# The MLP's 512-column products read and write backwards, and the sums' tiles begin elsewhere

## The chip, the cores and the metric

The kernel runs on one core of a Trainium2 chip. The metric is the device time of one execution in microseconds. A time is given as the median of several runs; a profile is of one execution, and its span reaches from the first to the last instruction of that execution.

## What is computed

The reference is one block of a network on 2048 positions of 640 channels. A condition `c` gives six modulation rows. A layer norm with two of them feeds a state-space convolution, done with Fourier transforms along the sequence; its output, gated, is added to `x`. A second layer norm feeds a gated MLP with 1728 hidden columns, and that output is gated and added again.

```python
x = A_u
mod = (_silu(c) @ w_mod).reshape(c.shape[0], 6, 1, -1)
sa, ca, ga, sb, cb, gb = (mod[:, i] for i in range(6))
h = _layernorm(x) * (1 + ca) + sa
x = x + ga * _A_ref(h, ...)              # convolution
h = _layernorm(x) * (1 + cb) + sb
gate, up = h @ w1, h @ w3                # 640 -> 1728
x = x + gb * ((_silu(gate) * up) @ w2)   # 1728 -> 640
return x
```

## The kernel before

**Two stages.** The first 380 us or so build the convolution's kernel and apply it; the change leaves them alone. After that the MLP runs to the end. Its tiles come from a pool `wq` in SBUF and two pools of PSUM banks of 512 fp32 columns, `psA` (five banks) and `psG` (three); the function `bank` hands them out under the name `ps`.

**Positions and weights.** The 2048 positions are four quarters of 512. Two quarters, "A" and "B", are worked on together, in two rounds (`pair`). A matmul has 128 rows of channels on the partitions, a stationary tile of 128 x 128 weights and a moving tile of 128 x 512, the quarter; its result is a whole bank of 128 x 512. The 640 channels are five blocks `k`; the 1728 hidden columns are 14 tiles `f`, the last of 64 columns, in which gate and up share one tile.

**Three matmuls for one product.** Every operand is split into a high and a low part (`split`, `x_split`, `w_split`: ScalarE casts to the rounded type `F32R`, VectorE takes the difference). `prod3` (line 1241) multiplies high with high, high with low and low with high, all adding up in one bank. These are the names in the trace: `gh`, `gl`, `uh`, `ul` for the parts of gate and up weights (the parts of `w2` and of the hidden tile use the same places), `xA`, `xB` and `T` for moving tiles, `S0h` to `S3l` for sums of weights.

**Strassen blocks.** `seven` computes, for one tile `f` and both quarters, gate and up together with seven block products in place of eight. Four of them need sums or differences of weights, made by `w_sums` (line 1307; GpSimd adds into `S0` to `S3`) and split by `w_split` (ScalarE into `S0h`.., VectorE into `S0l`..) for the next block while the present one is multiplied. Each is a tile of 128 partitions x 2 blocks x 128 columns, of which one block of 128 columns at a time is the stationary tile. `plain` does the tiles that are not done so: four tiles in the first round, one in the second, each for A and for B; the first of them uses an order of its own (`early`, line 1269 on).

**Output product.** `outputs` (line 1386 on) goes over the 14 hidden tiles of a quarter with five banks open. For four of them the hidden tile is stationary and 512 columns of `w2` move; for the fifth 128 columns of `w2` are stationary and the hidden tile moves (line 1455).

**What sets the order.** The program's order on an engine is kept where `in_order` is set or `keep_in_program_order` is called; elsewhere the framework's scheduler orders the instructions, and it puts in all waits. Places in SBUF are given out by the pools from the sizes of the tiles.

Not all 512-column matmuls are in the change: the `idle` ones of `keep_warm` (line 1054) and those of the first stage (line 541) are not.

Of the kernel before, what the change touches and what calls it, by code (L numbers as in the profile page):

```python
# [9 lines left out]
F32 = mybir.dt.float32  # L10
F32R = mybir.dt.float32r
# [6 lines left out]
P = 128  # L18
# [90 lines left out]
def tile_kernel(ctx: ExitStack, tc: tile.TileContext, a):  # L109
    nc = tc.nc  # L110
    V, S, G, PE = nc.vector, nc.scalar, nc.gpsimd, nc.tensor
# [725 lines left out]
    first, rest = Polar(d0, Vo, l2f), Polar(d1, Go, [l2, l2])  # L837
# [81 lines left out]
    for word in FRONT:  # L919
        main, *opts = word.split("/")  # L920
        n = next((int(o) for o in opts if o.isdigit()), 0)
        tag = next((o for o in opts if o in ("A", "B")), "B")
        name, k = main.split("+") if "+" in main else (main, None)
# [5 lines left out]
        else:  # L929
            k = int(k)  # L930
# [41 lines left out]
    for rnd in range(NS // EB + 3):  # L972
        for word in ROUND:
            word, _, idle = word.partition("/")
            name, k = word[:2].rstrip("+-"), EB * rnd + int(word[len(word[:2].rstrip("+-")):])
# [11 lines left out]
    for tk in range(NS - 4, LAG + 8 * NDC + 2):  # L987
        do("st", tk)
        do("kc", tk)
        last = do("iv", tk - 1)  # L990
# [11 lines left out]
        i = tk - 1 - LAG - 8 * NDC + 8  # L1002
# [31 lines left out]
    wq = ctx.enter_context(tc.tile_pool(name="wq", bufs=1, side="right"))  # L1034
    sp_order = [False]
    V, S, G, PE = (InOrder(tc, e, (in_order,)) for e in (V, S, G, PE))
# [204 lines left out]
    def prod3(ps, terms, first, last):  # L1241

        n = len(terms)
        for i, ((wh, wl), (xh, xl)) in enumerate(terms):
            for j, (w, x) in enumerate(((wh, xh), (wh, xl), (wl, xh))):
                ins = PE.matmul(ps, w, x, start=(first and i + j == 0), stop=(last and i == n - 1 and j == 2),
                                skip_group_check=not first)
        return ins

# [9 lines left out]
    def plain(c, f, h, ws, early=False, between=None, then=None):  # L1259

        last = f == NFT - 1
        wgs, wus = ws
        ks = range(KD) if c == "A" else (4, 0, 2, 3, 1)
        x = {k: xop[c, k] for k in ks}
        pg = bank(1)
        if early and f == 0:
            pu = bank(1)
            for lo in range(2):
                for k in range(KD):
                    for ps, ws in ((pg, wgs), (pu, wus)):  # L1270
                        for i in range(1 if lo else 2):
                            end = PE.matmul(ps, ws[i][:, k, :], x[k][lo], start=(k + i + lo == 0),
                                            stop=(lo == 1 and k == KD - 1))
        else:
            end = prod3(pg, [(wk(wgs, k), x[k]) for k in ks], True, True)
            if between:
                with tc.issue_after(end.ins):
                    between()
            if not last:
                pu = bank(1)  # L1280
                terms = [(wk(wus, k), x[k]) for k in ks]
                if then:
                    end = prod3(pu, terms[:3], True, True)
                    with tc.issue_after(end.ins):
                        then()
                    end = prod3(pu, terms[3:], False, True)
                else:
                    end = prod3(pu, terms, True, True)
        sg = room(8)
        if not last:  # L1290
            S.activation(sg, pg, AF.Silu)
            made[0] = V.tensor_tensor(h, pu, sg, op=OP.mult)
        else:
            S.activation(sg[:64], pg[:64], AF.Silu)
            made[0] = V.tensor_tensor(h[:64], pg[64:], sg[:64], op=OP.mult)
        return end
# [5 lines left out]
    def block_split(W):  # L1302
        W[2] = split(W[0], WS, ("gh", "gl"))
        W[3] = split(W[1], WS, ("uh", "ul"), part=slice(2, KD))
        return W

    def w_sums(W, names):

        wg, wu, _, _, sums = W
        for n in names:  # L1310
            t = (wq.tile([P, 2, P], F32, name=f"S{n}"), wq.tile([P, 2, P], F32R, name=f"S{n}h"),
                 wq.tile([P, 2, P], F32R, name=f"S{n}l"))
            raw = lambda i: sums[i][0]
            l, r = (lambda: (wu[:, :2], wu[:, 2:4]), lambda: (raw(0), wg[:, :2]),
                    lambda: (wg[:, :2], wu[:, :2]), lambda: (wg[:, 2:4], raw(1)))[n]()
            G.tensor_tensor(t[0], l, r, op=OP.subtract if n else OP.add)
            sums[n] = t
# [68 lines left out]
    def outputs(q0, order, hs, side, last):  # L1386


        seq = [(c, f) for c in range(2) for f in order]
        n_all, raws, ops, xr, accs, late = len(seq), {}, {}, [], [], []  # L1390

        def load(n):
            if n < n_all:
                raws[n] = weight(seq[n][1], "w2")

        def gate(n):

            if last and NFT <= n < n_all:
                V.tensor_tensor(raws[n][:, :512], raws[n][:, :512], gbr, op=OP.mult)

        def operands(n):
            if n < n_all:
                c, f = seq[n]
                ops[n] = out_operands(raws.pop(n), hs[c][f], f)

        def tail(tiles, ob, x, g):

            pt = bank(g)
            for i in tiles:
                PE.transpose(pt[:, i * P:(i + 1) * P], ob[:, i * P:(i + 1) * P], ident)  # L1410
            for i in tiles:
                V.tensor_tensor(x[i][:, 512:], pt[:, i * P:(i + 1) * P], x[i][:, 512:], op=OP.add)

        def finish(i, q, ob, x, gated, g):

            tail((i,), ob, x, g)
            V.tensor_tensor(x[i][:, :512], gated[i], x[i][:, :512], op=OP.add)
            x_out(4 * q + i, x[i])

        in_order[0] = True  # L1420
        for n in range(5):
            load(n)
        operands(0)
        in_order[0] = False
        yield
        in_order[0] = True
        for n, (c, f) in enumerate(seq):
            q, pos = q0 + c, n % NFT
            operands(n + 1)
            load(n + 5)  # L1430
            gate(n + 3)
            if pos == 10:
                xr = [x_tile(), x_tile()] + ([x_tile(), x_tile()] if c or last else [x_place("T41"), x_place("T31")])
                for i in range(4):
                    SQ.dma_start(xr[i], xs[4 * q + i])
            if pos == 0:
                acc = {k: bank(0) for k in (4, 0, 1, 2, 3)}
            side(n)
            terms = ops.pop(n)
            run = [(k, terms) for k in (4, 0, 1, 2, 3)]  # L1440

            if c and last and pos == NFT - 2:
                held, run = terms, run[:3]
            if c and last and pos == NFT - 1:
                run[3:] = [(k, held + terms) for k in (2, 3)]
            if pos == NFT - 1:
                if c == 0:
                    gated, ob = [room(4 + i) for i in range(4)], room(8)
                elif last:
                    ob = room(8)  # L1450
                else:
                    *gated, ob = places(3) + places(3)[:2]
            for k, terms in run:
                for i, (hh, w) in enumerate(terms):
                    lhs, rhs = (hh[:, k * P:(k + 1) * P], w[:, :512]) if k < 4 else (w[:, 512:], hh)
                    PE.matmul(acc[k], lhs, rhs, start=(pos == 0 and i == 0),
                              stop=(pos == NFT - 1 and i == len(terms) - 1))
                if pos < NFT - 1:
                    continue

                if k == 4:
                    S.activation(ob, acc[4], AF.Copy, scale=modT[:, 2, 4:5])
                elif not (c and last):
                    V.tensor_tensor(gated[k], acc[k], gbr, op=OP.mult)
                else:
                    V.tensor_tensor(xr[k][:, :512], acc[k], xr[k][:, :512], op=OP.add)
                    if k == 1:
                        tail(range(4), ob, xr, 1)
                    for i in ((), (0, 1), (2,), (3,))[k]:
                        x_out(4 * q + i, xr[i])  # L1470
            for t in late[:2]:
                t()
            late = late[2:]
            if pos == NFT - 1 and not (c and last):
                late = [lambda i=i, t=(q, ob, xr, gated, 1 - c): finish(i, *t) for i in range(4)]
        side(n_all)
        in_order[0] = False
        yield
        for t in late:
            t()  # L1480
            yield
# [58 lines left out]
    for pair in range(2):  # L1540
# [5 lines left out]
        ws = first_plain.pop() if first_plain else plain_weights(simple[0], last_sum)  # L1546
# [18 lines left out]
        for n, f in enumerate(simple):  # L1565
            hA[f] = h_tile()
            ws = ws or plain_weights(f, ends if pair == 0 and n == 1 else None)
            end = plain("A", f, hA[f], ws, pair == 0, *((lambda: turn(4, 0, 2), lambda: turn(3, 1)) if n == 3 else ()))
            if n < len(simple) - 1:
                ws = None  # L1570
# [111 lines left out]
```

## Time and profile before

| | us |
|---|---|
| median of three runs | 934.82 (934.5 to 937.22) |
| span of the profiled execution | 932.9 |
| TensorE busy | 894.6, 8482 matmuls |
| VectorE busy | 692.8 |
| ScalarE busy | 552.7 |
| GpSimd busy | 282.3 |

In the trace PE is TensorE's matmul, PEld its load of stationary weights (a row of its own, since it overlaps with matmuls), DVE VectorE, ACT ScalarE, POOL GpSimd and SP the queue of SyncE. A row of groups has the line, the engine, the operation, the tiles (written <- read, without buffer numbers), the shapes and the count; then busy time in us and the mean duration of one in ns; then idle time before them. All instructions that go through the helper which keeps the program's order have its line, L103, so that the tiles tell them apart. In a timeline the first number is the start and the second how long the row lasts. Matmuls are pipelined, and one's duration reaches into the next; the step from start to start is the time that each takes from the engine.

### The profile page before, as it was taken

What the parts mean: (1) busy time and instruction counts of PE and PEld (TensorE: products, weight loads), DVE (VectorE), ACT (ScalarE), POOL (GpSimd) and SP (SyncE); (2) the same over time, 40 slices, a digit from 0 to 9 for tenths busy, and PEclk for the clock granted to TensorE, in tenths of its full rate; (3) what the DMA queues carried; (4) which work ended last, traced back from release to release, by engine and by line L of the source; (5) the groups of instructions that cost most, each with busy time, mean ns of one, the idle gap of its engine ahead of it and who ended that gap; (6) DMA issues with size and microseconds to landing.
All of it is one profiled execution on the core that took longest, in us unless ns stands there. A gap on an engine that the chain in (4) does not pass through costs nothing.

```text
span 932.9 us, 21160 instructions
## 1 busy us (share of the span) xinstructions
PE 894.6 (96%) x8482; PEld 699.1 (75%) x8482; DVE 692.8 (74%) x1251; ACT 552.7 (59%) x810; POOL 282.3 (30%) x282
## 2 busy tenths in 40 slices
PE   5999889999999999999999999999999999999998
PEld 3776667767777766678888887778888888888886
DVE  6699889999999967676666656686876766664665
ACT  4899899999999843464433323466643333333432
POOL 3633465555556312134222200111632222200000
PEclk9999999999999999999999999999999999999999
DMA  8755888665655987853113117984322211203453
GB/s 253 243 198 201 264 230 223 171 162 153 177 155 149 230 223 245 211 212 99 56 49 97 55 45 201 271 258 158 86 70 85 84 57 57 57 29 99 141 169 114
DMA packets 103703, 140.79 MB, mean 151 GB/s; under 512 B 20612, under 2 KB 62788, under 8 KB 103604
## 3 DMA queue, kind: packets, MB, share of 16 engines
q1 hardware_dynamic: 99772, 129.32, 47.8%
q0 software_dynamic: 2368, 7.77, 2.6%
q10 hardware_dynamic: 1464, 2.34, 0.8%
q8 instruction: 67, 1.10, 0.5%
q14 instruction: 32, 0.26, 0.1%
HBM read 107.94 MB, written 31.46 MB: 149 GB/s over the span
## 4 chain that ended last, share of the span: by engine, by line
PE 72%; ACT 14%; DVE 5%; DMA 4%; issue 3%; SPq 1%; DVEq 0%; ACTq 0%
PE ps L103 56%; PE p L672 4%; ACT cs L137 3%; PE pz L721 3%; ACT A L137 3%; ACT ph L137 2%; PE pm L103 2%; ACT L137 2%; PE pk L614 1%; PE pq L552 1%; PE pa L541 1%; ACT kc L140 1%; DVE uk L103 1%; SPq L103 1%; ACT uk L140 1%
## 5 line engine op out<-in xcount | busy, mean ns | idle before, releaser
L103 DVE TENSOR_TENSOR s<-ps,s 128x512 f32<-128x512 f32 x138 | 94.9, 687 | 80.2 <-PE ps L103 79.7
L566 POOL TENSOR_TENSOR ph<-thi,iota 128x1024 int32<-128x1024 int32 x40 | 98.0, 2451 | 129.5 <-DVE A L604 77.5
L103 DVE TENSOR_TENSOR gl<-rw,gh 128x640 fp32r<-128x640 f32 x87 | 78.0, 897 | 64.2 <-ACT gh L103 64.2
L103 ACT CAST gh<-rw 128x640 fp32r<-128x640 f32 x87 | 63.3, 727 | 101.8 <-PE ps L103 61.5
L103 POOL TENSOR_TENSOR S<-rw 128x256 f32<-128x256 f32 x46 | 36.6, 798 | 170.7 <-DVE S0l L103 151.5
L103 PE MATMUL ps<-xA,gh 128*128 128x512 f32 x280 | 87.9, 392 | 0.1
L103 PE MATMUL ps<-gh,uh 128*128 128x512 f32 x224 | 87.5, 391 | 0.0
L103 PE MATMUL ps<-gl,uh 128*128 128x512 f32 x224 | 87.2, 389 | 0.0
L103 PE MATMUL ps<-gh,ul 128*128 128x512 f32 x208 | 81.1, 390 | 0.0
L672 PE MATMUL p<-uk,s 128*64 128x256 f32 x640 | 77.1, 383 | 0.9 <-issue 0.9
L103 PEld LDWEIGHTS ps<-xA,gh 128*128 128x128 f32 x280 | 52.1, 188 | 12.8 <-ACT xA L103 0.8
L672 PEld LDWEIGHTS p<-uk,s 128*64 128x64 f32 x640 | 43.4, 137 | 22.5 <-issue 3.4
L103 PE MATMUL ps<-xA,gl 128*128 128x512 f32 x140 | 54.5, 390 | 0.0
L103 ACT ACTIVATE s<-ps 128x512 f32<-128x512 f32 (+1 forms) x33 | 19.7, 598 | 50.5 <-PE ps L103 50.5
L600 DVE TENSOR_TENSOR A<-A,ph 128x1024 f32<-128x1024 f32 x40 | 49.0, 1226 | 0.0
L721 PE MATMUL pz<-Y,i 64*128 64x128 f32 x640 | 45.5, 281 | 3.6 <-ACT zt L140 2.0
L721 PEld LDWEIGHTS pz<-Y,i 64*128 64x128 f32 x640 | 39.3, 187 | 12.8 <-issue 7.3
L593 DVE TENSOR_TENSOR E<-A,cs 128x1024 f32<-128x1024 f32 x40 | 48.6, 1216 | 0.4
L103 PEld LDWEIGHTS ps<-gl,uh 128*128 128x128 f32 x224 | 42.1, 188 | 9.0
L103 PEld LDWEIGHTS ps<-gh,uh 128*128 128x128 f32 x224 | 42.1, 188 | 8.7
L137 ACT ACTIVATE cs<-cs,hp 128x1024 f32<-128x1024 f32 x40 | 45.3, 1153 | 0.2
L570 POOL TENSOR_TENSOR ph<-ph,phi 128x512 int32<-128x512 int32 x40 | 44.5, 1115 | 2.6
(244 smaller groups left out, 2301.6 us busy)
## 6 DMA issues: line engine op xcount, KB each, us to landing
rw<-in_w_dram SPq DMA_DIRECT2D x52, 320.0 KB, 3.0
us<-u SPq DMA_DIRECT2D x16, 640.0 KB, 4.5
s<-in_s_dram SPq DMA_DIRECT2D x40, 256.0 KB, 3.4
i<-in_i_dram SPq DMA_DIRECT2D x40, 256.0 KB, 4.0
rw<-in_wg_dram SPq DMA_DIRECT2D x31, 320.0 KB, 3.0
rw<-in_wu_dram SPq DMA_DIRECT2D x28, 320.0 KB, 3.5
uk<-us SPq DMA_DIRECT2D x32, 256.0 KB, 8.1
zs<-zt SPq DMA_DIRECT2D x32, 256.0 KB, 4.1
```

The lines of the kernel that those rows point to most:

```text
L103: ins = fn(*args, **kw)
L137: return tc.keep_in_program_order(S.activation(*args, **kw))
L140: return tc.keep_in_program_order(S.copy(out, in_))
L541: keep(PE.matmul(pA[s][:, rr, :], la[r, t, :], r2[r, js, :].rearrange("p j b -> p (j b)"), start=True, stop=True, tile_position=(r.start, 0)))
L552: keep(PE.matmul(pQ[s][:, rr, :256], w[r, t, :], bc(sel[r, js], 2, NA) if i else r1[r, js, :], start=(i == 0), stop=(i == 1), tile_positio ...
L566: keep(G.tensor_tensor(p, bc(thi[:, s * SD:s * SD + SD], 2, NPH), bc(iota, 1, SD), op=OP.mult))
L570: keep(G.tensor_tensor(p[:, :, :NA], p[:, :, :NA], bc(phi[:, s * SD:s * SD + SD], 2, NA), op=OP.add))
L593: keep(V.tensor_tensor(EC[s][:, :, 1:3, :], AA[s][:, :, 1:3, :], mid(cs[s]), op=OP.mult))
L600: keep(V.tensor_tensor(A[:, :, 1:3, :], A[:, :, 1:3, :], mid(ph[s]), op=OP.mult))
L614: keep(PE.matmul(pk[dq * 32:dq * 32 + 32, g, :], x[:, g * 4 + dq, 1, :], x[:, g * 4 + dq, 0:3:2, :], start=(st == 0), stop=(st == 1), tile ...
L672: keep(PE.matmul(p2[par * 64:par * 64 + 64, pi, c, :], s2[:, pi * 2 + par, c * 64:c * 64 + 64], uk[:, 0:kn + 1:kn, f, :], start=True, stop ...
L721: ins = keep(PE.matmul(pz[:, par, (g % 2) * 2 + pi, :], i1[r, pi, c, :], Y[r, pi, c, :], start=(c == 0), stop=(c == 1), tile_position=(par ...
```

## The change

In three places, a matmul's output and its moving operand are given with a step of -1 along the columns, `[:, ::-1]`: in `prod3`, in the early part of `plain` and in `outputs`. The last column is read and written first. The result of each column lies where it lay before.

In `w_sums` the eight split tiles of the sums are made by a new function, `shifted`. The table `ROOM` gives for each a number of columns by which the tile is made wider, and the column at which its 256 columns begin. The tile of the unsplit sum is as before.

```diff
-                ins = PE.matmul(ps, w, x, start=(first and i + j == 0), stop=(last and i == n - 1 and j == 2),
+                ins = PE.matmul(ps[:, ::-1], w, x[:, ::-1], start=(first and i + j == 0), stop=(last and i == n - 1 and j == 2),
                                 skip_group_check=not first)
...
-                            end = PE.matmul(ps, ws[i][:, k, :], x[k][lo], start=(k + i + lo == 0),
+                            end = PE.matmul(ps[:, ::-1], ws[i][:, k, :], x[k][lo][:, ::-1], start=(k + i + lo == 0),
                                             stop=(lo == 1 and k == KD - 1))
...
+    ROOM = {"S0h": (8, 1), "S0l": (0, 0), "S1h": (8, 2), "S1l": (0, 0), "S2h": (24, 4), "S2l": (0, 0), "S3h": (40, 0),
+            "S3l": (8, 3)}
+
+    def shifted(name):
+
+        extra, at = ROOM[name]
+        t = wq.tile([P, 2 * P + extra], F32R, name=name)
+        return t[:, at:at + 2 * P].rearrange("p (k c) -> p k c", k=2)
+
     def w_sums(W, names):
...
-            t = (wq.tile([P, 2, P], F32, name=f"S{n}"), wq.tile([P, 2, P], F32R, name=f"S{n}h"),
-                 wq.tile([P, 2, P], F32R, name=f"S{n}l"))
+            t = (wq.tile([P, 2, P], F32, name=f"S{n}"), shifted(f"S{n}h"), shifted(f"S{n}l"))
...
-                    PE.matmul(acc[k], lhs, rhs, start=(pos == 0 and i == 0),
+                    PE.matmul(acc[k][:, ::-1], lhs, rhs[:, ::-1], start=(pos == 0 and i == 0),
                               stop=(pos == NFT - 1 and i == len(terms) - 1))
```

## The prediction

> **What bounds the kernel now.** I read the head of the page, its chain, then the table of windows, the merged chain in order of time, and last the timeline of TensorE inside the last stage.
>
> ```profile
> span 932.9 us, 21160 instructions
> PE 894.6 (96%) x8482; PEld 699.1 (75%) x8482; DVE 692.8 (74%) x1251; ACT 552.7 (59%) x810; POOL 282.3 (30%) x282
> ...
> PE 72%; ACT 14%; DVE 5%; DMA 4%; issue 3%; SPq 1%; DVEq 0%; ACTq 0%
> ```
>
> ```profile
> 500.00:550.00 50.00, 50.00 (x222) 41.42 (x221) 32.27 (x58) 18.89 (x36) 8.89 (x12) 1.00 0.19 54
> 600.00:650.00 50.00, 50.00 (x284) 38.28 (x283) 37.68 (x72) 31.86 (x49) 7.67 (x13) 1.00 0.70 209
> 800.00:850.00 50.00, 50.00 (x223) 41.40 (x222) 27.97 (x46) 17.13 (x31) 2.95 (x4) 1.00 0.19 54
> ```
>
> ```profile
> 416.61 244.49 PE ps L103 x1163
> 661.75 267.25 PE ps L103 x1182
> ```
>
> The last 530 us are one stretch of TensorE work. In the windows the first time after the width is TensorE's busy time, 50.00 of 50 us, at a granted clock of 1.00 (third column from the end), and the merged chain from 416.61 to 929.00 us holds almost nothing but matmuls into the tiles `ps`. VectorE (32.27, 37.68 and 27.97 us of 50) and ScalarE are well below that. So whatever the change does to the time of a 512-column product goes straight into the end; whatever it does to the other engines has to be large to be seen.
>
> How long is one product? Not what the groups give as a mean of one (that is its latency, and neighbours overlap), but the step from one start to the next:
>
> ```profile
> 789.68 0.39 PE L103 MATMUL ps<-xA,gl 128*128 128x512 f32 x1
> 789.90 0.62 PE L103 MATMUL ps<-xA,gh 128*128 128x512 f32 x2
> 790.36 0.39 PE L103 MATMUL ps<-xA,gl 128*128 128x512 f32 x1
> 790.58 0.62 PE L103 MATMUL ps<-T,S0h 128*128 128x512 f32 x2
> 791.04 0.39 PE L103 MATMUL ps<-T,S0l 128*128 128x512 f32 x1
> 791.26 0.62 PE L103 MATMUL ps<-T,S0h 128*128 128x512 f32 x2
> 791.72 0.39 PE L103 MATMUL ps<-T,S0l 128*128 128x512 f32 x1
> 791.94 0.62 PE L103 MATMUL ps<-xB,uh 128*128 128x512 f32 x2
> 792.40 0.39 PE L103 MATMUL ps<-xB,ul 128*128 128x512 f32 x1
> ```
>
> Twelve products start between 789.68 and 792.40: 2.72 / 12 = 226.7 ns a step, the same for `gh`, `uh` and the sums `S0`. The reader is to see that nothing in it wobbles: while VectorE and ScalarE work at two thirds and one third of their time, and transfers run, the step stays the same. Any gain must come out of the step itself.
>
> **How many products the edit touches.** Seven Strassen products a weight block are 54 matmuls (seven of two terms and four of one term more, each term three matmuls), for 23 blocks: 1242. The plain blocks are 240, and the output product 4 x (13 x 15 + 10) = 820. Together **2302**. The 32 `idle` matmuls (line 1054) and the transposes are not touched. 2302 x 226.7 ns is 521.9 us, 56% of the span. One nanosecond a product is 2.3 us, and 0.3% of the kernel is 1.2 ns a product.
>
> **The change, part by part.** It adds no instruction, no transfer and no wait: the same matmuls in the same accumulations, with first and last column exchanged in reading and in writing, so every column meets the same weights. No engine gets another queue. What moves is where a stream begins: at the last column of `x`, `h` or `w2` and of its bank of PSUM, while the load of the next weights begins, as before, at its first.
>
> *Read and write from behind.* The trace of before has no matmul with a descending operand, so this is an unknown, to be bounded. Another engine does read descending in this kernel: lines 596 and 604 take `cs` and `ph` with a step of -1, lines 593 and 600 with +1.
>
> ```profile
> L600 DVE TENSOR_TENSOR A<-A,ph 128x1024 f32<-128x1024 f32 x40 | 49.0, 1226 | 0.0
> L593 DVE TENSOR_TENSOR E<-A,cs 128x1024 f32<-128x1024 f32 x40 | 48.6, 1216 | 0.4
> L596 DVE TENSOR_TENSOR E<-A,cs 128x512 f32<-128x512 f32 x40 | 28.5, 712 | 0.0
> L604 DVE SCALAR_TENSOR_TENSOR A<-ph,A 128x512 f32<-128x512 f32 x40 | 27.5, 702 | 0.0
> ...
> L103 DVE TENSOR_TENSOR s<-ps,s 128x512 f32<-128x512 f32 x138 | 94.9, 687 | 80.2 <-PE ps L103 79.7
> ```
>
> 712 and 702 ns descending stand beside 687 ns for 512 ascending columns (from PSUM): 15 to 25 ns an instruction, none of it a doubling. That speaks against a catastrophe, though VectorE's ports need not be TensorE's.
>
> For the gain, the nearest row is the one stream in the trace that sends 512 columns in another form: line 672, two 64-column halves side by side, 256 columns each.
>
> ```profile
> 249.59 1.95 PE L672 MATMUL p<-uk,s 128*64 128x256 f32 x16
> ```
>
> ```profile
> L672 PE MATMUL p<-uk,s x640: 379/379/431, 129.6 to 362.6; 128*64 128x256 f32 x160
> ```
>
> Sixteen matmuls are eight pairs, 512 columns a pair; less one duration (431 or 379 ns) the 1.95 us leave 1.52 to 1.57 us for seven steps, **217 to 224 ns**. So TensorE passes 512 columns and turns to new weights in 2.7 to 10 ns less than the 226.7 ns of the MLP. Some of that step is a turn-over between two instructions, and not streaming; and the turn-over is what the edit touches, since it moves both ends of every stream. Bounds a product: -10 ns (all of it gone, -23.0 us) on the one side; on the other +6 ns, the spread of the durations of one such product (389 to 395 ns in the row of S1h below), +13.8 us. Between them I take **-3.3 ns**, a third of the 10: nearer to the row of the MLP itself, since a step that is alike for every tile gives no sign that all of it can go. 2302 x 3.3 = **7.6 us** less, all of it on the path.
>
> [...]
>
> *The eight places.* Five of the eight tiles grow, together by 88 elements of 4 bytes in each partition, four begin 1, 2, 4 or 3 elements behind their start, and tiles laid out behind them in the same pool move.
>
> ```profile
> L103 PEld LDWEIGHTS ps<-T,S1h x92: 187/188/188, 439.4 to 824.6; 128*128 128x128 f32 x92
> L103 PE MATMUL ps<-T,S1h x92: 389/389/395, 439.6 to 824.8; 128*128 128x512 f32 x92
> L103 ACT CAST S1h<-S x23: 403/406/408, 427.6 to 813.1; 128x256 fp32r<-128x256 f32 x23
> L103 DVE TENSOR_TENSOR S1l<-S,S1h x23: 408/415/626, 428.0 to 813.9; 128x256 fp32r<-128x256 f32 x23
> ```
>
> A load of these weights takes 188 ns inside a step of 226.7: 38.7 ns are cover, and only what a load from a skew start takes beyond that reaches the path. The sums are 4 x 46 x 3 = 552 of the loads; were they late by 4 ns (nothing shows it), that would be 2.2 us. The casts and differences that write the tiles are done 11 us ahead of their first use (428.0 and 0.4 beside 439.4), so even twice their 0.4 us stays hidden; that cover gone, each of the 23 blocks would pay up to 0.4 us a sum. I cost the places at nothing beyond what they share in the step.
>
> **Sum.** 932.9 - 7.6 = 925.3 us of span. The median of the runs, 934.82, lies 1.9 us above the profiled span; the forecast is 925.3 + 1.9, **927 us**.
>
> **The rivals.**
>
> *Same step.* The turn-over belongs to the exchange of weights in the array and does not see where a stream begins. For it: 226.7 ns for every operand in the timeline above, in and out of the sums. Against it: line 672 turns over faster in the same array, so the turn-over does hang on an instruction's operands. Time: 934.8, give or take 2. The same comes out if the patterns are undone on their way to the chip.
>
> *A dearer step (the other side).* The first columns come late: the stream begins at the end of a row, and reads or writes that profit from going up lose it at each start. Place: the start of each of the 2302 products; price: the 6 ns by which one product may last longer (395 against 389), 13.8 us, **949 us**. It decides from 1.2 ns a product on. For it: VectorE's descending instructions cost 15 to 25 ns more than the ascending one. Against it: VectorE's pair also differs in where its operands lie (PSUM or SBUF), so these may be no price of direction.
>
> *A stream at half speed.* If each descending column takes two slots of the stream in place of one, a product costs up to 226.7 ns more: 2302 x 226.7 = 522 us, some 1457 us. Against it: VectorE's 712 beside 687 ns.
>
> [...]
>
> **How the numbers follow.** Forecast (a shorter step): 0.47, with its own range 911 to 931. Same step: 0.20. Dearer step: 0.28, half speed: 0.05. What a measurement of this kernel can tell from no change is about 0.3%, 2.8 us. Faster by more 0.47, within 0.20, slower by more 0.33. The range reaches from 910 (a little past the whole 10 ns) to 951 (a little past the 6 ns more); I leave some 0.04 below it and 0.14 above.
>
> **What would show it.** In the profile of the changed kernel, the step between starts in the timeline around 790 us: 223 ns by the forecast, 226.7 by the same step, 233 by the dearer, over 400 by half speed; and with it the number of matmuls in the windows of 50 us at full TensorE (222 or 223 now; 225 or 226 by the forecast). If the places matter by themselves, the steps into S0 to S3 differ from those into `gh` and `uh`; if the loads suffer, their 188 ns grow. The forecast is wrong if the step is unchanged and time goes elsewhere: into waits of TensorE on S tiles, or into the first 380 us, which the edit leaves alone.

## The result, and the profile after

| | before | after |
|---|---|---|
| median of the runs, us | 935.66 (934.5 to 937.22, 4 runs) | 947.57 (946.58 to 947.97, 4 runs) |
| span of the profiled execution, us | 932.9 | 946.2 |

The ratio is 1.0133, with a 95% interval of 1.0116 to 1.0149: **slower by 1.3%**, where 927 us had been forecast. In the MLP every engine works through the same instructions in the same order in both profiles.

Two windows of the changed kernel (columns as before: PE, PEld, DVE, ACT, POOL busy with counts, granted clock, share and rate of the transfers), and the end of its merged chain:

```profile
500.00:550.00 50.00, 50.00 (x215) 40.23 (x214) 31.42 (x56) 18.26 (x37) 9.44 (x13) 1.00 0.17 54
800.00:850.00 50.00, 50.00 (x215) 40.23 (x214) 29.91 (x50) 16.85 (x32) 5.88 (x8) 1.00 0.13 39
```

```profile
416.25 526.09 PE ps L103 x2347
```

TensorE is as full as before and its clock is granted as before, but 215 matmuls fit into 50 us where 222 and 223 did. From 416 us on, the same matmuls last 526.1 us in place of 512.4 (416.61 to 929.00), 13.7 us more; the span grew by 13.3. So all of it came from this stretch. The timeline of TensorE in the changed kernel:

```profile
799.77 0.40 PE L103 MATMUL ps<-xA,gl 128*128 128x512 f32 x1
800.01 0.63 PE L103 MATMUL ps<-T,S0h 128*128 128x512 f32 x2
800.47 0.40 PE L103 MATMUL ps<-T,S0l 128*128 128x512 f32 x1
800.71 0.63 PE L103 MATMUL ps<-T,S0h 128*128 128x512 f32 x2
801.17 0.40 PE L103 MATMUL ps<-T,S0l 128*128 128x512 f32 x1
801.41 0.63 PE L103 MATMUL ps<-xB,uh 128*128 128x512 f32 x2
801.87 0.40 PE L103 MATMUL ps<-xB,ul 128*128 128x512 f32 x1
802.11 0.63 PE L103 MATMUL ps<-T,S2h 128*128 128x512 f32 x2
802.57 0.40 PE L103 MATMUL ps<-T,S2l 128*128 128x512 f32 x1
```

Twelve starts in 2.80 us: **233.3 ns a step**, 6.7 ns more than in the timeline of the forecast. Over all products, leaving out the few steps above 300 ns, the mean step is 227.2 ns before and 233.6 after, which is why the 13.7 us are a little less than 2302 x 6.7 = 15.4. The loads of the weights did not grow, those from a tile that begins 8 bytes later among them:

```profile
L103 PEld LDWEIGHTS ps<-T,S1h x92: 188/188/188, 439.7 to 835.1; 128*128 128x128 f32 x92
L103 PE MATMUL ps<-T,S1h x92: 395/398/400, 439.9 to 835.3; 128*128 128x512 f32 x92
```

The steps into the sums differ from the others only a little: products of S1 step by some 235 ns and those of `S3l` by 238, all of it together some 0.4 us.

### The profile page after: what moved, and what is told of

It is laid out like the page before. It is cut to its first block, busy times and chain, and to the rows that moved or that the text cites. A ratio compares the mean times of both kernels' runs of the same rounds, so it can differ in the third digit from the quotient of the medians.

```text
span 946.2 us, 21160 instructions
## 1 busy us (share of the span) xinstructions
PE 906.7 (96%) x8482; PEld 698.8 (74%) x8482; DVE 693.0 (73%) x1251; ACT 552.0 (58%) x810; POOL 277.5 (29%) x282
## 4 chain that ended last, share of the span: by engine, by line
PE 75%; ACT 12%; DVE 7%; issue 3%; DMA 2%; POOL 0%; DVEq 0%; POOLq 0%; ACTq 0%
PE ps L103 58%; PE p L672 5%; PE pz L721 3%; ACT cs L137 3%; ACT A L137 2%; ACT ph L137 2%; PE pk L614 2%; DVE uk L103 2%; ACT L137 1%; PE pm L103 1%; PE pt L633 1%; PE pa L541 1%; PE pq L552 1%; ACT kc L140 1%; DVE E L593 1%
## 5 line engine op out<-in xcount | busy, mean ns | idle before, releaser
L103 DVE TENSOR_TENSOR gl<-rw,gh 128x640 fp32r<-128x640 f32 x87 | 76.0, 874 | 69.3 <-ACT gh L103 69.2
L103 PE MATMUL ps<-xA,gh 128*128 128x512 f32 x280 | 89.9, 400 | 0.1
L103 PEld LDWEIGHTS ps<-gh,ul 128*128 128x128 f32 x208 | 39.1, 188 | 9.4
```

Source lines behind the costliest of these rows:

```text
L103: ins = fn(*args, **kw)
```

## The experiments

### Which part of the change

**The places alone** (`e1_places`): the change without its three reversals.

> The eight places alone; all products stream forwards. Direction theory (the backward stream costs 6.7 ns a product, the places next to nothing): about 935 us, step 226.7 ns everywhere except a few ns more into the shifted sums. Address theory (the step is set by where operands start within 64 bytes; the five wider tiles move every tile of the pool from 32 to 0 modulo 64): the step changes for all products, up or down, and the time with it by 2.3 us per ns.

Measured: 939.67 us, ratio 1.0059 (1.0042 to 1.0076). The timeline around products of a sum:

```profile
785.79 0.62 PE L103 MATMUL ps<-xB,gh 128*128 128x512 f32 x2
...
789.87 0.62 PE L103 MATMUL ps<-T,S1h 128*128 128x512 f32 x2
790.32 0.40 PE L103 MATMUL ps<-T,S1l 128*128 128x512 f32 x1
790.56 0.63 PE L103 MATMUL ps<-T,S1h 128*128 128x512 f32 x2
791.02 0.40 PE L103 MATMUL ps<-T,S1l 128*128 128x512 f32 x1
791.26 0.62 PE L103 MATMUL ps<-xA,gh 128*128 128x512 f32 x2
...
792.63 0.62 PE L103 MATMUL ps<-xA,gh 128*128 128x512 f32 x2
```

Up to 789.87 eighteen products step by 226.7 ns; from there the next twelve need 2.76 us, 230 ns each, and the six behind the last product of S1 are among them (1.37 us, 228 ns each). The places do cost time when the stream goes forwards, 5.3 us by the medians, and they cost it in the stream, though the loads of `S1h` still take 187 to 189 ns.

**The reversal alone** (`e2_reversed`): the three lines with `[:, ::-1]`, tiles as before.

> The backward stream alone; all tiles where they were (32 modulo 64). Direction theory: the step is 233.3 ns everywhere, about 949 us. Address theory: another step than 233.3, since the streams now start at 28 and not at 60 modulo 64 and the weights at 32 and not at 0; anything from 216 to 240 ns, 911 to 966 us.

Measured: 947.61 us, ratio 1.0145 (1.0128 to 1.0162), 216 matmuls in each of the two windows. That is the whole of the change's loss: with the places 1.0133, without them 1.0145, the intervals overlap. The step is the direction's, with the tiles of the change or without them, and the 5 us of the places are not added to it.

**All tiles moved by 32 bytes** (`e3_pad`): one tile is 8 columns wider, so that the pool should lay its tiles elsewhere. The profiles show no addresses; where the tiles lie is worked out from their sizes, here and in the next two runs.

```diff
-                 wq.tile([P, 2, P], F32R, name=f"S{n}l"))
+                 wq.tile([P, 2 * P + 8 * (n == 3)], F32R, name=f"S{n}l")[:, :2 * P].rearrange("p (k c) -> p k c", k=2))
```

> The kernel before with S3l alone 8 columns wider and begun at its first column: every tile of the pool moves by 32 bytes, from 32 to 0 modulo 64, nothing else changes. Direction theory: no change, 935 us. Address theory: another step for all products; by the turn-over seen in line 672 it may fall to 217 to 224 ns, 913 to 929 us.

Measured: 934.25 us, ratio 0.9997 (0.998 to 1.0014). Moving them all together is of no account, if they moved as worked out.

**Which property of the places.** `e10_widths` keeps the wider tiles and begins each at its first column (`return t[:, :2 * P]`); `e11_starts` has the starts of the change, but widths of 0 or 16 columns, so that every tile stays on the old grid of 64 bytes.

> The places alone, forwards, with the wider tiles but all begun at their first column: the sums' weights lie at 0 or 32 bytes modulo 64, no other start. If the 5 us of the places alone came from starts off the 32-byte grid: 934 us. If a change of 32 bytes between one load of weights and the next is enough to unsettle the forward stream: 937 to 940 us, with steps above 230 ns at the products of sums.

> The skew starts alone, forwards: every tile is 64 bytes wider or not at all, so that all tiles stay 32 modulo 64, and only S0h, S1h, S2h and S3l begin 4, 8, 16 and 12 bytes behind. If the skew starts unsettle the forward stream: 937 to 940 us, steps above 230 ns at products of these four, 226.7 elsewhere. If the widths did it: 934 us.

Measured: 937.48 us, ratio 1.0032 (1.0016 to 1.0047), and 939.61 us, ratio 1.0089 (1.005 to 1.0129). Both cost something, 3.5 and 5.6 us by the medians; the runs of the second scatter up to 951.8 us, which lifts its ratio above that of its medians, 1.006. The time is lost around the products of sums: in the profiles the eight kinds of them step by 228 to 235 ns on average in both kernels, where all eight stood at 226.5 to 226.9 before, and the other products by 228 as against 227; the last 1182 products of TensorE's chain take 269.32 and 270.05 us, where 267.25 stood before. In the second kernel the low parts, whose tiles begin where they began, are slower too (232 and 233 ns for `S1l` and `S0l`, which were expected at 226.7). That would fit with a price for every change of the start from one load of weights to the next; this is my guess, and how such a change would reach the stream, no run shows.

**Reading or writing.** `e5_write` turns only the outputs round, `e6_read` only the moving tiles.

```diff
+                ins = PE.matmul(ps[:, ::-1], w, x, ...     # e5_write
+                ins = PE.matmul(ps, w, x[:, ::-1], ...     # e6_read
```

> Only the output of the 2302 products is written backwards; the moving tiles are read forwards (so the columns of every product come out mirrored). Read theory (the dearer step belongs to reading the moving tile backwards): the step is 226.7 ns and the time 934 us. Write theory (it belongs to PSUM): 233.3 ns and 948 us.

> Only the moving tiles are read backwards; PSUM is written forwards (columns mirrored again). Read theory: 233.3 ns, 948 us. Write theory: 226.7 ns, 934 us. If each half costs a part, both kernels lie between.

Measured: 934.49 us for writing (ratio 1.002, 0.9978 to 1.0063) and 948.76 us for reading (1.0135, 1.0065 to 1.0204). The same window of each:

```profile
800.00:850.00 50.00, 50.00 (x223) 41.38 (x222) 28.05 (x46) 16.92 (x31) 2.95 (x4) 1.00 0.17 54
```

```profile
800.00:850.00 50.00, 50.00 (x216) 40.26 (x215) 30.37 (x51) 17.18 (x32) 5.86 (x8) 1.00 0.14 40
```

223 matmuls as before when only PSUM is written backwards, 216 when only SBUF is read backwards. All of the loss is in reading. (A product that is turned round on one side alone has its columns mirrored, so these two kernels do not compute the block.)

**A part of the products** (`e8_outputs`): the third reversal alone, 820 products.

> Backwards in the output product alone, 820 of the 2302 products, places as before. If each backward product costs 6.7 ns on TensorE's path, wherever it stands: 820 x 6.7 = 5.5 us more, 940 us. If the cost arose through the pipelines of the Strassen blocks: no change, 934 us.

Measured: 939.63 us, ratio 1.005 (1.0018 to 1.0082), 5.7 us above its runs of before; the interval leaves room for 1.7 to 7.7 us. Its profile is sharper: the products of the output step by 233 ns or a little more, and those of the Strassen blocks by 227 as before. The price goes with each product.

### What in the reading costs the time

**Ten products, many starts** (`e4_bench`).

> The kernel before with 84 groups of ten 512-column matmuls on zeros ahead of the MLP, each group with another start of the moving tile (M, bytes modulo 64) and of the stationary tile (S), forwards (u) or backwards (d) in reading and writing. Direction theory: all groups uu step alike, about 226.7 ns, all dd alike, about 233. Address theory: the step goes with M and S; groups with one direction spread by several ns, and M32S32uu shows 226.7, M60S0dd 233.3. The mixed groups (ud, du) tell reading from writing.

Backwards in both, nineteen of the twenty groups stepped by 233 ns, whatever their starts; forwards, groups differed. Some rows of its timeline (start, length of the whole group):

```profile
399.48 2.43 PE L189 MATMUL M32S8uu<-T 128*128 128x512 f32 x10
...
436.48 2.47 PE L189 MATMUL M32S32uu<-T 128*128 128x512 f32 x10
...
496.66 2.50 PE L189 MATMUL M60S0dd<-T 128*128 128x512 f32 x10
```

2.43 us less a last duration of 0.39 are nine steps of 226.7 ns, 2.50 less 0.40 nine of 233.3. Ten products proved too few to tell a start from the settling of the stream: M32S32uu, the case of the kernel before, has not reached 226.7 here. It is inconclusive on the starts, and led to groups of thirty.

**Columns, weights, types** (`e7_bench`).

> The kernel before with groups of thirty matmuls on zeros ahead of the MLP: N columns (512, 384, 256), weights of W columns (128, 64, 32), forwards (U) or backwards (D), then two-byte and full fp32 operands, and two groups that write backwards. Cost per stream (the extra arises at a start): D minus U is 6.7 ns at every N. Cost per column: 6.7, 5.0 and 3.3 ns at 512, 384 and 256. [...]

The timeline, from which the step is the distance from one group's start to the next's, by 30:

```profile
381.60 6.96 PE L133 MATMUL N512W128U<-T 128*128 128x512 f32 x30
388.40 7.17 PE L133 MATMUL N512W128D<-T 128*128 128x512 f32 x30
395.41 7.07 PE L133 MATMUL N512W64U<-T 128*64 128x512 f32 x30
402.31 7.17 PE L133 MATMUL N512W64D<-T 128*64 128x512 f32 x30
409.31 7.11 PE L133 MATMUL N512W32U<-T 128*32 128x512 f32 x30
416.26 7.17 PE L133 MATMUL N512W32D<-T 128*32 128x512 f32 x30
...
439.03 5.43 PE L133 MATMUL N384W64D<-T 128*64 128x384 f32 x30
444.30 5.37 PE L133 MATMUL N384W32U<-T 128*32 128x384 f32 x30
...
454.77 3.77 PE L133 MATMUL N256W128U<-T 128*128 128x256 f32 x30
458.38 3.72 PE L133 MATMUL N256W128D<-T 128*128 128x256 f32 x30
461.93 3.59 PE L133 MATMUL N256W64U<-T 128*64 128x256 f32 x30
465.36 3.70 PE L133 MATMUL N256W64D<-T 128*64 128x256 f32 x30
468.90 3.57 PE L133 MATMUL N256W32U<-T 128*32 128x256 f32 x30
...
475.84 6.65 PE L133 MATMUL SHORTW128U<-T 128*128 128x512 bf16 x30
482.33 6.64 PE L133 MATMUL SHORTW128D<-T 128*128 128x512 bf16 x30
...
501.97 26.02 PE L133 MATMUL FULLW128U<-T 128*128 128x512 f32 x60
527.82 25.91 PE L133 MATMUL FULLW128D<-T 128*128 128x512 f32 x60
```

Backwards with 64 columns of weights the steps are 233.3, 175.7 and 118.0 ns for 512, 384 and 256 columns: 57.7 ns for every 128 columns and some 2.6 ns beside them. So a backward stream is paid by the column, and at 512 columns it does not depend on the weights: 7.17 us with 128, 64 and 32 columns of them. D minus U does shrink with the weights (some 7, 3 and 2 ns at 512 columns), as a collision of the stream with the load of the next weights might have it, but since U grows (226.7, 230.0, 231.7 ns) and not because D falls. Forwards there is no such simple line: with 256 columns and 128 of weights U is even dearer than D (120.3 against 118.3 ns). So D minus U, which is what the change paid, follows neither of the two rows that were expected for it, one price per stream or one per column: with 128 columns of weights it is 7 ns at 512 columns, some 3 at 384 and -2 at 256. Of the two groups that write backwards, the one that reads backwards too takes 7.17 us like the others that do, 233.7 ns from start to start (7.01 / 30). The one that reads forwards, first behind the full fp32 groups, takes 7.38 us and 240.7 ns on average (7.22 / 30), so that for writing alone `e5_write` is the better witness.

And two-byte operands know no direction (6.65 and 6.64 us, (6.65 - 0.38) / 29 = 216 ns a step), nor does full fp32, of which the trace lists two passes for each matmul (x60 for thirty): 431 ns a pass (25.85 / 60), the groups lasting 26.02 and 25.91 us. The theory of one price at each start falls, and a collision with the load of the next weights does not show in D, which is the same with 128, 64 and 32 columns of them; of the three types only four-byte operands in a single pass (x30 for thirty) lose by going backwards. No run leaves the loads of weights out, so what part they have in the forward step stays open.

**Other orders of the same columns** (`e9_patterns`).

> The kernel before with groups of thirty matmuls on zeros ahead of the MLP, all with four-byte operands, 512 columns read in other orders: blocks taken from behind with ascending columns inside (BLOCKSDOWN), blocks in order with descending columns inside (INSIDEDOWN), two halves or four quarters in turns (HALVES, QUARTERS), one column again and again (SAME), every second column (STEPTWO), one row of 128 four times (SAMEROW). If the extra comes from fetching the moving tile: SAME falls to the 215.8 ns of two-byte operands, STEPTWO is far above 233, and the orders fall into 226.7 or 233.3 ns by the size of the block at which the direction turns. If it is a rate of the array itself with four-byte operands: SAME stays at 226.7 ns and all orders lie at 226.7 to 233.3. An order below 226.7 ns would beat both kernels.

```profile
388.28 7.17 PE L137 MATMUL DOWNA<-T 128*128 128x512 f32 x30
395.28 7.16 PE L137 MATMUL BLOCKSDOWN2X<-T 128*128 128x512 f32 x30
...
437.11 6.96 PE L137 MATMUL BLOCKSDOWN128X<-T 128*128 128x512 f32 x30
443.91 6.96 PE L137 MATMUL INSIDEDOWN2X<-T 128*128 128x512 f32 x30
...
464.49 8.16 PE L137 MATMUL INSIDEDOWN16X<-T 128*128 128x512 f32 x30
...
493.59 6.64 PE L137 MATMUL HALVES1X<-T 128*128 128x512 f32 x30
500.07 10.17 PE L137 MATMUL HALVES2X<-T 128*128 128x512 f32 x30
...
574.62 6.72 PE L137 MATMUL SAMEA<-T 128*128 128x512 f32 x30
581.18 13.78 PE L137 MATMUL STEPTWOA<-T 128*128 128x512 f32 x30
```

The same products cost from 6.64 to 13.78 us for thirty by nothing but the order in which columns are read. Descending blocks of two cost as much as a stream backwards, descending blocks of 128 nothing; descending pairs inside ascending blocks cost nothing, sixteens inside cost most (266.7 ns). Every second column doubles the step (453.3 ns), and one column again and again takes 218.7. So the step is no fixed rate of the array for four-byte operands. But the orders do not fall into the two steps 226.7 and 233.3 either, as had been expected if it is the fetch, and what rule they follow stays open. And one order is quicker than the kernel before: column 0, 256, 1, 257 and so on, 6.48 / 30 = **216 ns**.

**In turns from two halves, in the kernel** (`e12_turns`). The matmuls read so and write PSUM in order; the last operation behind each product puts the columns back.

```diff
+    turns = lambda v: v.rearrange("p (a c) -> p c a", a=2)
+    paired = lambda v: v.rearrange("p (c a) -> p c a", a=2)
+    halves = lambda v: v.rearrange("p (a c) -> p a c", a=2)
+    back = lambda v: v.rearrange("p (c a) -> p a c", a=2)
...
-                ins = PE.matmul(ps, w, x, start=(first and i + j == 0), stop=(last and i == n - 1 and j == 2),
+                ins = PE.matmul(paired(ps), w, turns(x), start=(first and i + j == 0), stop=(last and i == n - 1 and j == 2),
...
-        V.tensor_tensor(hB, t, c12, op=OP.mult)
+        V.tensor_tensor(halves(hB), back(t), back(c12), op=OP.mult)
...
-                    S.activation(ob, acc[4], AF.Copy, scale=modT[:, 2, 4:5])
+                    S.activation(halves(ob), back(acc[4]), AF.Copy, scale=modT[:, 2, 4:5])
-                    V.tensor_tensor(gated[k], acc[k], gbr, op=OP.mult)
+                    V.tensor_tensor(halves(gated[k]), back(acc[k]), halves(gbr), op=OP.mult)
```

(The other two matmuls, the other products of `seven` and `plain` and the last sum are edited alike.)

> All 2302 products read their moving tile in turns from its two halves (columns 0, 256, 1, 257, ...) and write PSUM in order; the last elementwise operation behind each product puts the columns back. Fetch theory (the step above 215.9 ns is time to fetch four-byte columns): step 215.9 ns, 2302 x 10.8 ns = 24.9 us less than before, 909 us. Turn-over theory (it belongs to the exchange of weights): 226.7 ns, 934 us or some us more for the operations that put columns back.

Measured: **910.38 us** (908.7 to 912.19, 6 runs), ratio 0.9734 (0.9709 to 0.9759). A window, and the last stretch of the chain:

```profile
800.00:850.00 50.00, 50.00 (x234) 43.83 (x233) 26.79 (x39) 18.30 (x30) 0.00 (x0) 1.00 0.28 85
```

```profile
668.73 236.18 PE ps L103 x1097
```

```profile
L103 DVE TENSOR_TENSOR h<-s,s 128x512 f32<-128x512 f32 x24 | 16.4, 683 | 3.1 <-ACT s L103 3.0
L103 DVE TENSOR_TENSOR h<-s,s 128x512 f32<-128x512 f32 x24 | 20.9, 871 | 3.1 <-ACT s L103 3.0
```

234 matmuls in the window, and 236.18 us for the last 1097, 215 ns each: the step of two-byte operands, with every load of weights still there. So the turn-over theory falls. Putting the columns back lengthens VectorE's product of the hidden tile from 683 (first row, the kernel before) to 871 ns (second row), nearly all of it beside work that TensorE covers: it is busy for 49.4 us or more of each 50 from 450 to 900. This kernel beats both.

**With the eight places on top** (`e13_turns_places`), and **more places in turn** (`e14_turns`).

> The same, with the eight places of the change. If the places cost only because they disturb a fetch that is at its limit: no difference to the run without them, 909 us. If the load of weights from skew starts is itself late: some 3 to 5 us more.

> The kernel before with groups of thirty matmuls on zeros ahead of the MLP, read in turns from 2, 4, 8 and 16 places, upwards (U) and downwards (D). Fetch theory, with direction told by neighbours in the stream: in turns no neighbour lies next in memory, so U and D step alike, 215.9 ns at 2. If the direction is told by the whole pattern: D is dearer by up to 6.7 ns. More places may step like 2 or lose again.

The first took 912.63 us, ratio 0.9759 (0.9731 to 0.9786), 2.3 us more by the medians, with an interval that overlaps with the one without the places; its last 1097 products need 236.19 us where the other needs 236.18, so the stream does not see the places. In the second:

```profile
390.27 6.64 PE L116 MATMUL TURNS2UP<-T 128*128 128x512 f32 x30
396.75 6.64 PE L116 MATMUL TURNS2DP<-T 128*128 128x512 f32 x30
403.23 8.66 PE L116 MATMUL TURNS4UP<-T 128*128 128x512 f32 x30
411.72 8.77 PE L116 MATMUL TURNS4DP<-T 128*128 128x512 f32 x30
```

From two halves in turns, upwards and downwards step alike. Four places are slower than a plain stream (283 ns), eight and sixteen slower still (489 and 433 ns), and I have no explanation for that.

## Why the prediction was wrong

**What bounds the kernel: right.** The step of the 512-column products was the only term that moved the end, and the reading of it by start to start, the count of 2302 and the price of 2.3 us a ns hold within what was measured (`e8_outputs`: 820 products, 5.5 us expected, 5.7 measured).

**The step that failed** is the one that took the shorter step of line 672 for a quicker turn-over: "the turn-over is what the edit touches, since it moves both ends of every stream", and from it -3.3 ns. Line 672 multiplies full fp32, not the single-pass four-byte type of the MLP. `e7_bench` has some 430 ns for a pass of 512 columns of that type, in both directions; a pass of 256 columns would be half of it, an estimate of 215 ns. The trace of before bears that out: the starts of the two matmuls of a pair lie 6 to 7 ns apart, and the next pair starts 215 to 216 ns after the last, but for the first step of 267 ns. So the two halves of a pair run side by side, each for the full time of 256 such columns; the 217 to 224 ns were this time with the long first step in the mean, and no stream of 512 columns. And the step of the MLP holds no turn-over of 10 ns: with the same loads and the same exchanges of weights, `e12_turns` steps by 215 to 216 ns. That answers the rival of the same step too, which gave these 10 ns to the exchange of weights. What lies between 216 and 226.7 ns goes away when only the order changes in which four-byte columns are read; I call it time to fetch them, which is a name: no run shows the fetch by itself. Backwards the stream costs 57.7 ns for 128 columns (`e7_bench`). The edit lengthened what the forecast thought it might shorten.

**The rival of the dearer step** had sign and size (6 ns and 949 us, against 6.7 ns and 947.6 us), but not the place: it put the price at the start of each product, and in `e7_bench` the time of the backward stream goes by the column, with 2.6 ns beside. The row from which its 6 ns came (389 to 395 ns) was a spread of one product in the kernel before and told nothing of direction, so that the size came out is luck. The same holds for VectorE's 712 beside 687 ns: it pointed the right way, and no run connects it with TensorE's read.

**Half speed** did not come: the step grew by 6.7 ns, not by 226.7. Nor did the writing slow it: `e5_write` writes the columns of PSUM descending at no cost that its interval shows (0.9978 to 1.0063).

**The 216 ns.** That is the step of two-byte operands in `e7_bench` and of four-byte ones read in turns, with which the kernel of `e12_turns` lands on 910.4 us, at the low end of the forecast's range; a plain stream of four-byte columns takes 226.7 ns. The 910 came by another order of reading, and not by a cured turn-over.

**The places, costed at nothing:** right within the change, but the reason given does not carry it. The cover of 38.7 ns was never touched, the loads stay at 188 ns; all the same the places alone cost 0.6%, since the forward stream slows around the sums (230 ns a step from the first product of S1 in `e1_places`), a cost that the forecast did not have. Backwards next to nothing of it is left, and in turns nothing in the stream; why, no run shows.

## What to carry to other kernels

When TensorE is full, measure the step from start to start and compare it with that of another operand type in the same trace before it is called overhead: here 11 of 227 ns hung on the order of reading. The order in which the moving tile's columns are read is a free choice that was worth 3% of the step one way and 5% the other; single-pass four-byte operands read in turns from two halves ran at the two-byte rate (216 ns). A trial of thirty matmuls on zeros in front of the real work, with a name for each form, prices such choices in one run.

## What the runs showed of the hardware

- A 512-column product of single-pass four-byte operands steps by 226.7 ns forwards, 233.3 backwards, 216 in turns from two halves, 333 in turns by pairs, 453 at every second column (`e7_bench`, `e9_patterns`). How these numbers come about stays open; one column read again and again takes 218.7 ns, more than two halves in turns, so it is not the number of different columns alone.
- Forwards, with 128 columns of weights, groups of thirty stepped by 226.7 ns (`e7_bench`), groups of ten by 226.7 to 236 (2.43 to 2.52 us in `e4_bench`, the first group aside). With the tiles of the sums wider or begun later (`e10_widths`, `e11_starts`) their products stepped by 228 to 235 ns on average. Backwards nineteen of the twenty groups of `e4_bench`, with different starts, held 233.3 ns.
- The direction in which PSUM is written made no difference in `e5_write` (223 matmuls in the window both ways).
